# Narrow expert pieces: two groups of columns share a PSUM bank and one operation

## The chip, the cores and the metric

The kernel runs on one core of a Trainium2 chip. The metric is the device time of one execution in microseconds (us); the median of three runs before the change is 583.29 us (580.64 to 585.85). TensorE is called PE here, VectorE DVE, ScalarE ACT, GpSimd POOL; SP issues most of the DMAs.

## The reference

Three stages follow each other. First, attention inside chunks of 64 tokens, for 2 batches, 8 heads, 576 tokens and head size 64; its output is 1152 tokens of 512 numbers. Second, a mixture of 8 experts: each token goes to the one expert with the largest logit, at most 288 tokens to an expert, and gets `gate * (relu(x @ w1[e]) @ w2[e])` with w1 of 512x1024 and w2 of 1024x512. Third, a dense mixture of 4 domains: every token gets the sum over domains of `p[e] * (relu(x @ w1[e]) @ w2[e])`, with weights of the same sizes.

```
for i in range(N):
    e = expert_idx[i]
    if counts[e] < capacity:
        disp[e, counts[e]] = x[i]
...
h = np.maximum(np.einsum('ecd,edf->ecf', disp, w1), 0.0)
y = np.einsum('ecf,efd->ecd', h, w2)
```

With the inputs of these runs the 8 experts get 0, 210, 384, 0, 64, 174, 192 and 128 tokens.

## The kernel before, in words

All products are made from two parts of each number: a rounded high part and the remainder (low part). ACT writes the high part and DVE subtracts it from the number to get the remainder. For weights these are `part_hi` (L113, ACT, a cast of 128x1024) and `part_lo` (L117, DVE, a subtraction of 128x1024); a weight matrix half is one of four buffers `raws[j]`, `hls[j]`, each handled in two halves. Buffers 0 and 2 hold the two halves of w1, buffers 1 and 3 those of w2. So each expert costs eight casts on ACT and eight subtractions on DVE, and SP reloads a half of `raws` as soon as its subtraction is done.

The experts are worked one after another, as pieces, largest first, and each piece has a width in columns (tokens). Widths above 192 go through `wide`, with three matmuls for each product; widths 192 and 128 go through `joined`, where one matmul streams the high and low parts side by side (two halves of a bank) and a second adds the product of the weights' remainder. In these runs there are two wide pieces (k = 0 and 1), two pieces of width 192 (k = 2 and 3) and two of width 128 (k = 4 and 5). The last two are the narrow pieces. Then the dense stage begins with `first_dense` (L732 to L736) and takes most of the span.

A joined piece has a first layer of 8 groups of 4 matmul pairs (w1) and a second of 4 output groups with two halves each, 8 steps of 4 matmul pairs (w2). For each finished group `join` copies one half of the bank out on ACT (L626) and adds the other on DVE (L627), and `leave` clips the sum on ACT (L632) and takes the remainder on DVE (L633); in the second layer `leave` splits the result into `x2` (L546, L547). A result is left one group later than it is joined. Six banks rotate over the groups.

The order of the instructions on PE, ACT, DVE and SP is written out by hand. `chores` fills numbered slots, one after each of the 16 steps of a piece: `part_hi`, `part_lo` and `load` for the weights to come, `turn` (four PE transposes of the next expert's tokens into `tps`) and `split` (L546, L547 on them). Each engine executes its own list in order. Branches on the counted sizes choose the form of each next piece, so ACT and DVE jump to another piece of code when the form changes.

Of the kernel before, what the change touches and what calls it, by code (L numbers as in the profile page):

```python
# [20 lines left out]
P = 128  # L21
# [49 lines left out]
def kernel(ctx: ExitStack, tc: tile.TileContext, kqv_d, wg, w_all, dp, cst, out, cap):  # L71
# [461 lines left out]
    with ExitStack() as est:  # L533
# [8 lines left out]
        parts = [xtp.tile([P, CW], F32, name=f"part{j}") for j in range(3)]  # L542
        sums = [xtp.tile([P, CW], F32, name=f"sum{j}") for j in range(3)]
# [62 lines left out]
        def joined(k, W, slots):  # L606
# [5 lines left out]

            def bank(i):
                return banks[(first + i) % NB][:, 0:2 * W].rearrange("p (a n) -> p a n", a=2)
# [9 lines left out]
            def join(i):  # L624
                o, part, total = bank(i), parts[i % 3][:, 0:W], sums[i % 3][:, 0:W]
                nc.scalar.copy(part, o[:, 1])  # L626
                nc.vector.tensor_tensor(out=total, in0=o[:, 0], in1=part, op=ALU.add)  # L627

            def leave(i):
                total = sums[i % 3][:, 0:W]  # L630
                if i < NH * NF:
                    nc.scalar.activation(out=ht[:, i, 0], in_=total, func=ACTF.Relu)  # L632
                    nc.vector.scalar_tensor_tensor(out=ht[:, i, 1], in0=total, scalar=0.0, in1=ht[:, i, 0].bitcast(F32),  # L633
                                                   op0=ALU.max, op1=ALU.subtract)
                else:
                    d = i - NH * NF
                    hi_lo(x2[:, 0, d, cols], x2[:, 1, d, cols], total)

            def out(i):
                if i < last:  # L640
                    join(i)
                if i in range(1, last + 1) and i != NH * NF:
                    leave(i - 1)
# [7 lines left out]
            leave(NH * NF - 1)  # L651
            for h in range(NH):
                for d in range(KD):
                    for j in range(NF):
                        products(bank(NH * NF + d), lambda a: w2(h, a, j)[:, d * P:d * P + P], ht[:, NF * h + j],
                                 h == 0 and j == 0, h == NH - 1 and j == NF - 1)
                    if h == NH - 1:
                        out(NH * NF + d)
                    place(NH * NF + h * KD + d)
            leave(last - 1)  # L660

        def late(k):

            for h in range(2):
                part_hi(1, h)
# [351 lines left out]
```

## Time and profile before

| | |
|---|---|
| median of 3 runs | 583.29 us (580.64 to 585.85) |
| the profiled execution | 581.8 us, of which span 580.0 us |
| attention and routing | 0 to 64.6 us of the span |
| wide pieces, k = 0 and 1 | 64.6 to 117.8 us |
| pieces of 192 columns, k = 2 and 3 | 117.8 to 158.4 us |
| narrow pieces, k = 4 and 5 | 158.4 to 195.1 us |
| dense stage | 195.1 to 580 us |
| busy share of the span | PE 96%, DVE 53%, ACT 33% |

The boundaries are the starts of the first matmul of each piece in PE's order of time. PE is busy for nearly all of the span, so a change shows in the time where PE stands still, or where its clock is low.

### The profile page before, as it was taken

To read this page: it belongs to the slowest core of one execution; us is meant where nothing else is said; L and a number is where in the kernel's file an instruction comes from. 1 tells how busy PE (TensorE), PEld (TensorE's weight loads), DVE (VectorE), ACT (ScalarE), POOL (GpSimd) and SP (SyncE) were. 2 spreads that over 40 slices of the span, in tenths; PEclk is the share of its full clock that TensorE was granted. 3 is DMA by queue.
4 is the path that set the end of the run, shared out by engine and by line. 5 is a ranking of instruction groups with operands and counts; after the bars stand their busy time and mean duration, and the time that the engine had idled before them with its cause. 6 is when DMAs were issued, how large, how long until landed. Compare 5 with 4: busy or idle time off the path is not lost.

```text
span 580.0 us, 9331 instructions
## 1 busy us (share of the span) xinstructions
PE 557.7 (96%) x3627; PEld 510.3 (88%) x3627; DVE 305.2 (53%) x657; ACT 192.8 (33%) x429; POOL 64.3 (11%) x57
## 2 busy tenths in 40 slices
PE   7999799999989899999999999999999999999994
PEld 4786699999978788898898899899899889889984
DVE  5998576569868744334433524524533533453221
ACT  5785135568767541022122122122111212211110
POOL 3321805401103000000000000000000000000032
PEclk9999899999999899999999999999999999999999
DMA  8881394657748824011201202101210000000022
GB/s 333 316 289 62 87 366 149 201 177 250 239 147 273 257 66 160 1 37 41 69 3 70 73 0 73 56 18 38 73 36 2 1 0 1 0 1 1 1 92 76
DMA packets 17012, 59.99 MB, mean 103 GB/s; under 512 B 2768, under 2 KB 2912, under 8 KB 16288
## 3 DMA queue, kind: packets, MB, share of 16 engines
q1 hardware_dynamic: 14688, 52.91, 26.9%
q0 software_dynamic: 2240, 6.09, 3.2%
q8 instruction: 37, 0.61, 0.4%
q14 instruction: 47, 0.39, 0.2%
HBM read 54.25 MB, written 4.75 MB: 102 GB/s over the span
## 4 chain that ended last, share of the span: by engine, by line
PE 86%; DVE 6%; issue 3%; DMA 1%; ACT 1%; POOL 1%; SPq 0%; POOLq 0%; DVEq 0%; ACTq 0%
PE pg L863 31%; PE po L892 22%; PE po L911 9%; PE bank L579 9%; PE bank L617 5%; PE bank L618 2%; DVE hl L117 2%; PE bank L732 2%; PE w_ps L143 1%; PE s_ps L212 1%; DMA kqv<-in_kqv 1%; PE tp L552 1%; PE o_ps L234 1%; PE lr_ps L262 1%; DVE sum L627 1%
## 5 line engine op out<-in xcount | busy, mean ns | idle before, releaser
L863 PE MATMUL pg<-x,hl 128*128 128x384 f32 (+1 forms) x1104 | 181.1, 323 | 1.3 <-DVE htb L735 1.3
L863 PEld LDWEIGHTS pg<-x,hl 128*128 128x128 f32 x1104 | 178.0, 188 | 2.8 <-ACT htb L734 1.6
L117 DVE TENSOR_TENSOR hl<-raw,hl 128x1024 fp32r<-128x1024 f32 x80 | 96.8, 1220 | 8.7 <-ACT hl L113 8.7
L113 ACT CAST hl<-raw 128x1024 fp32r<-128x1024 f32 x80 | 82.0, 1049 | 4.1 <-issue 3.0
L892 PE MATMUL po<-hl,htb 128*128 128x512 f32 x288 | 68.4, 395 | 0.0
L892 PE MATMUL po<-hl,h_other 128*128 128x512 f32 (+1 forms) x300 | 68.4, 386 | 0.0
L892 PEld LDWEIGHTS po<-hl,h_other 128*128 128x128 f32 x300 | 54.6, 188 | 11.8
L892 PEld LDWEIGHTS po<-hl,htb 128*128 128x128 f32 x288 | 53.9, 188 | 12.1
L899 DVE SCALAR_TENSOR_TENSOR xr<-po,mcol,xr 128x512 f32<-128x512 f32 (+1 forms) x43 | 31.7, 738 | 58.2 <-PE po L892 57.5
L873 ACT ACTIVATE h_other<-pg 128x384 fp32r<-128x384 f32 x32 | 15.5, 490 | 90.1 <-PE pg L863 90.1
L873 ACT ACTIVATE htb<-pg 128x384 fp32r<-128x384 f32 x28 | 13.7, 491 | 87.0 <-PE pg L863 87.0
L874 DVE SCALAR_TENSOR_TENSOR h_other<-pg,h_other 128x384 fp32r<-128x384 f32 x32 | 17.6, 557 | 43.7 <-ACT h_other L873 43.7
L874 DVE SCALAR_TENSOR_TENSOR htb<-pg,htb 128x384 fp32r<-128x384 f32 x28 | 15.6, 558 | 43.7 <-ACT htb L873 43.7
L617 PE MATMUL bank<-htb,hl 128*128 128x384 f32 (+1 forms) x128 | 35.9, 355 | 0.1
L617 PE MATMUL bank<-xt,hl 128*128 128x384 f32 (+1 forms) x128 | 33.8, 348 | 1.9 <-DVE xt L547 1.0
L618 PE MATMUL bank<-htb,hl 128*128 128x192 f32 (+1 forms) x128 | 30.7, 240 | 1.2 <-DVE hl L117 1.2
L407 POOL DMA_INDIRECT xr<-x_d,gidx x18 | 21.5, 1195 | 85.5 <-PE tp L552 62.4
L920 POOL MEMSET raw<- 128x512 f32 x1 | 0.5, 525 | 272.8 <-DVE hl L117 272.8
L618 PE MATMUL bank<-xt,hl 128*128 128x192 f32 (+1 forms) x128 | 30.3, 237 | 0.0
L579 PE MATMUL bank<-xt,hl 128*128 128x232 f32 (+1 forms) x192 | 25.4, 296 | 2.9 <-issue 2.9
L579 PEld LDWEIGHTS bank<-xt,hl 128*128 128x128 f32 x192 | 25.1, 202 | 3.0 <-issue 3.0
L917 DVE TENSOR_TENSOR rest<-po,rest 128x288 f32<-128x288 f32 x28 | 12.8, 457 | 26.7 <-PE po L911 26.7
(174 smaller groups left out, 694.8 us busy)
## 6 DMA issues: line engine op xcount, KB each, us to landing
raw<-in_w_all SPq DMA_DIRECT2D x72, 512.0 KB, 4.7
kqv<-in_kqv SPq DMA_DIRECT2D x8, 768.0 KB, 7.6
raw<-in_w_all SPq DMA_DIRECT2D x4, 1024.0 KB, 5.5
x_d<-x SPq DMA_DIRECT2D x9, 256.0 KB, 2.8
xt<-meta_d SPq DMA_DIRECT2D x1, 1056.0 KB, 8.8
kqv<-in_kqv SPq DMA_DIRECT2D x3, 256.0 KB, 2.9
ca<-in_cst SPq DMA_DIRECT2D x1, 320.0 KB, 7.8
xr<-x_d,gidx POOLq DMA_INDIRECT x18, 5.5
```

What stands on the lines that cost most here:

```text
L113: nc.scalar.copy(hls[j][:, 0, a:b], raws[j][:, a:b])
L117: nc.vector.tensor_tensor(out=hls[j][:, 1, a:b], in0=raws[j][:, a:b], in1=hls[j][:, 0, a:b].bitcast(F32), op=ALU.subtract)
L407: nc.gpsimd.indirect_dma_start(out=xrs[k % 2][0:n, w, :], out_offset=None, in_=x_d[:, :], in_offset=bass.IndirectOffsetOnAxis(ap=ix, axis=0))
L579: nc.tensor.matmul(o, wt(a), t[:, b, 0:W], start=start and i == 0, stop=stop and i == len(PAIRS) - 1, skip_group_check=True)
L617: nc.tensor.matmul(o, wt(0), t[:, :, 0:W], start=start, stop=False, skip_group_check=True)
L618: nc.tensor.matmul(o[:, 0], wt(1), t[:, 0, 0:W], start=False, stop=stop, skip_group_check=True)
L863: nc.tensor.matmul(pg[:, 0:n], w1(u % 2, a, kd)[:, ff * P:ff * P + P], x2[:, b, kd, g * GW:g * GW + n], start=c == 0, stop=c == 3 * KD - 1)
L873: nc.scalar.activation(out=h[:, ff, 0], in_=pg[:, 0:GW], func=ACTF.Relu)
L874: nc.vector.scalar_tensor_tensor(out=h[:, ff, 1], in0=pg[:, 0:GW], scalar=0.0, in1=h[:, ff, 0].bitcast(F32), op0=ALU.max, op1=ALU.subtract)
L892: nc.tensor.matmul(po, h[:, ff, a, tt * P:tt * P + P], w2(u % 2, b, ff)[:, cols], start=c == 0, stop=c == 3 * NF - 1)
L899: nc.vector.scalar_tensor_tensor(out=acc[t][:, cols], in0=po, scalar=pe, in1=acc[t][:, cols], op0=ALU.mult, op1=ALU.add)
L911: nc.tensor.matmul(po[:, 0:W], w2(u % 2, b, ff)[:, d * P:d * P + P], h[:, ff, a, 0:W], start=c == 0, stop=c == 3 * NF - 1)
```

## The change

For pieces of 128 columns (`DW`), `joined` is called with m = 2: two groups of columns are put into one PSUM bank, and one copy, one sum, one clip and one remainder serve both, on 128x256 elements. So a narrow piece uses its six banks once each. The next expert's transposes are done two at a time into one bank, and their split is one operation for both (`turn2`, `split2`). Since two groups of the second layer lie in one bank, its eight steps get another order. For pieces of 192 columns (m = 1) `joined` computes as before. In every piece but the first, the casts and subtractions of the w2 halves are put into other slots: casts after steps 0, 1, 3 and 5 where they stood after 0, 2, 5 and 7, subtractions after 0, 2, 4 and 6 where they stood after 1, 3, 6 and 8.

```diff
-            def join(i):
-                o, part, total = bank(i), parts[i % 3][:, 0:W], sums[i % 3][:, 0:W]
-                nc.scalar.copy(part, o[:, 1])
-                nc.vector.tensor_tensor(out=total, in0=o[:, 0], in1=part, op=ALU.add)
+                nc.scalar.copy(kept(parts, i), half(i, 1))
+                nc.vector.tensor_tensor(out=kept(sums, i), in0=half(i, 0), in1=kept(parts, i), op=ALU.add)
...
             def out(i):
-                if i < last:
-                    join(i)
-                if i in range(1, last + 1) and i != NH * NF:
-                    leave(i - 1)
+                if (i + 1) % m:
+                    return
+                i += 1 - m
+                join(i)
+                if i and i != NH * NF:
+                    leave(i - m)
...
+            steps = [(h, d) for h in range(NH) for d in range(KD)]
+            if m > 1:
+                steps = [(0, 0), (0, 2), (1, 0), (0, 1), (1, 1), (1, 2), (0, 3), (1, 3)]
...
+            def turn2(kd):
+                for i in range(2):
+                    xturn(k + 1, kd + i, tps[kd // 2][:, i * W:], W)
+
+            def split2(kd):
+                t = tps[kd // 2][:, 0:2 * W].rearrange("p (b n) -> p b n", b=2)
+                hi_lo(*(xts[(k + 1) % 2][:, kd:kd + 2, a, 0:W] for a in range(2)), t)
+
+            if k + 1 < NE and W == DW:
+                for kd in (0, 2):
+                    at(7 + kd, turn2, kd)
+                    at(8 + kd, split2, kd)
...
-                    at((0, 2, 5, 7)[n], part_hi, j, h)
-                    i = (1, 3, 6, 8)[n]
+                    at((0, 1, 3, 5)[n], part_hi, j, h)
+                    i = (0, 2, 4, 6)[n]
```

How the instructions move on DVE, at the start of a narrow piece. `sum` rows are joins, `htb` rows are the remainders of the clipped result, `hl1` and `hl3` rows are the subtractions for the two halves of w2. Before:

```order
L627 TENSOR_TENSOR sum0_1054<-bank0_1042,part0_1051 128x128
L627 TENSOR_TENSOR sum1_1055<-bank1_1043,part1_1052 128x128
L633 SCALAR_TENSOR_TENSOR htb_1035<-sum0_1054,htb_1035 128x128
L117 TENSOR_TENSOR hl1_94<-raw1_90,hl1_94 128x1024
L627 TENSOR_TENSOR sum2_1056<-bank2_1044,part2_1053 128x128
L633 SCALAR_TENSOR_TENSOR htb_1035<-sum1_1055,htb_1035 128x128
L627 TENSOR_TENSOR sum0_1054<-bank3_1045,part0_1051 128x128
L633 SCALAR_TENSOR_TENSOR htb_1035<-sum2_1056,htb_1035 128x128
L117 TENSOR_TENSOR hl1_94<-raw1_90,hl1_94 128x1024
L627 TENSOR_TENSOR sum1_1055<-bank4_1046,part1_1052 128x128
```

And now:

```order
L117 TENSOR_TENSOR hl1_94<-raw1_90,hl1_94 128x1024
L635 TENSOR_TENSOR sum0_1054<-bank0_1042,part0_1051 128x256
L117 TENSOR_TENSOR hl1_94<-raw1_90,hl1_94 128x1024
L635 TENSOR_TENSOR sum1_1055<-bank1_1043,part1_1052 128x256
L642 SCALAR_TENSOR_TENSOR htb_1035<-sum0_1054,htb_1035 128x2x128
L117 TENSOR_TENSOR hl3_96<-raw3_92,hl3_96 128x1024
L635 TENSOR_TENSOR sum2_1056<-bank2_1044,part2_1053 128x256
L642 SCALAR_TENSOR_TENSOR htb_1035<-sum1_1055,htb_1035 128x2x128
L117 TENSOR_TENSOR hl3_96<-raw3_92,hl3_96 128x1024
L635 TENSOR_TENSOR sum0_1054<-bank3_1045,part0_1051 128x256
L642 SCALAR_TENSOR_TENSOR htb_1035<-sum2_1056,htb_1035 128x2x128
L642 SCALAR_TENSOR_TENSOR htb_1035<-sum0_1054,htb_1035 128x2x128
```

A weight subtraction now stands ahead of the first join, and all four of them stand among the first layer's four joins and four remainders.

On DVE at the end of a narrow piece, after the first layer's last remainder (`xt1` rows are the split of the next expert's tokens, `hl0` and `hl2` the next expert's w1, `x2` rows the piece's result). Now:

```order
L547 TENSOR_TENSOR xt1_1050<-tp0_1048,xt1_1050 128x2x128
L117 TENSOR_TENSOR hl0_93<-raw0_89,hl0_93 128x1024
L547 TENSOR_TENSOR xt1_1050<-tp1_1049,xt1_1050 128x2x128
L117 TENSOR_TENSOR hl0_93<-raw0_89,hl0_93 128x1024
L635 TENSOR_TENSOR sum1_1055<-bank4_1046,part1_1052 128x256
L117 TENSOR_TENSOR hl2_95<-raw2_91,hl2_95 128x1024 x2
L635 TENSOR_TENSOR sum2_1056<-bank5_1047,part2_1053 128x256
L547 ISA
L547 TENSOR_TENSOR x2_1032<-sum1_1055,x2_1032 128x2x128
L547 ISA
L547 TENSOR_TENSOR x2_1032<-sum2_1056,x2_1032 128x2x128
```

Before, this stretch held four splits of the tokens, four joins and four splits of the result, and the last split of the tokens stood behind the third split of the result. The next expert's tokens are now complete before the piece's first output group is joined.

## Rows read from the trace of the kernel before

**Rows 1.** Windows of the narrow pieces: engine busy times, PEclk (1.00 is full), DMA.

```profile
158.40:177.90 19.50, 16.81 (x134) 15.68 (x134) 14.26 (x33) 12.55 (x33) 1.29 (x1) 1.00 0.55 175
177.90:195.10 17.20, 15.75 (x134) 15.27 (x134) 15.26 (x37) 13.43 (x37) 4.57 (x3) 1.00 0.88 254
```

**Rows 2.** Timeline of PE, 158 to 212 us: its waits; start, length, instruction, idle.

```profile
165.16 0.38 PE L617 MATMUL bank<-xt,hl 128*128 128x256 f32 x1 [0.94 <-DVE sum L627]
...
169.11 0.33 PE L618 MATMUL bank<-htb,hl 128*128 128x128 f32 x1 [0.75 <-DVE hl L117]
...
173.50 0.33 PE L552 MATMUL tp<-cc,xr 128*128 128x128 f32 x1 [0.70 <-DVE xt L547]
...
179.78 0.36 PE L617 MATMUL bank<-xt,hl 128*128 128x256 f32 x1 [1.01 <-DVE xt L547]
...
196.23 1.31 PE L732 MATMUL bank<-x,hl 128*128 128x384 f32 x6 [0.71 <-DVE x L547]
...
198.42 9.01 PE L732 MATMUL bank<-x,hl 128*128 128x384 f32 x41 [0.88 <-DVE x L547]
```

**Rows 3.** Timeline of PE in the first narrow piece: two first matmuls, 21 pairs apart.

```profile
158.92 0.34 PE L617 MATMUL bank<-xt,hl 128*128 128x256 f32 x1
...
163.82 0.34 PE L617 MATMUL bank<-xt,hl 128*128 128x256 f32 x1
```

**Rows 4.** Timeline of ACT and DVE where the code changes form (k = 1 to 2, 3 to 4).

```profile
121.12 0.32 ACT L626 COPY part<-bank 128x192 f32<-128x192 f32 x1 [2.66 <-PE bank L618]
...
160.28 0.35 ACT L546 CAST x<-sum 128x192 f32 x1 [0.96 <-DVE sum L627]
...
160.66 0.36 DVE L547 TENSOR_TENSOR x<-sum,x 128x192 f32 x1 [0.16 <-ACT x L546]
...
164.01 0.27 ACT L626 COPY part<-bank 128x128 f32<-128x128 f32 x1 [3.38 <-PE bank L618]
...
164.82 0.29 DVE L627 TENSOR_TENSOR sum<-bank,part 128x128 f32<-128x128 f32 x1 [3.79 <-ACT part L626]
```

**Rows 5.** Groups by line and form: count, busy us, mean ns of one, idle before.

```profile
L117 DVE TENSOR_TENSOR hl<-raw,hl 128x1024 fp32r<-128x1024 f32 x80 | 96.8, 1220 | 8.7 <-ACT hl L113 8.7
L113 ACT CAST hl<-raw 128x1024 fp32r<-128x1024 f32 x80 | 82.0, 1049 | 4.1 <-issue 3.0 <-DMA raw<-in_w_all 1.1
...
L627 DVE TENSOR_TENSOR sum<-bank,part 128x128 f32<-128x128 f32 x24 | 6.9, 287 | 6.5 <-ACT part L626 6.5
...
L243 DVE TENSOR_TENSOR x<-o_ps,rs 128x256 f32<-128x256 f32 x18 | 6.8, 419 | 0.3
...
L256 ACT COPY xt<-et_ps 128x256 f32<-128x256 f32 x1 | 0.4, 378 | 0.0
```

**Rows 6.** Timeline of DVE: starts of operations that follow each other without idle time.

```profile
22.48 0.76 DVE L243 TENSOR_TENSOR x<-o_ps,rs 128x256 f32<-128x256 f32 x2
...
172.95 0.29 DVE L633 SCALAR_TENSOR_TENSOR htb<-sum,htb 128x128 fp32r<-128x128 f32 x1 [0.18 <-ACT htb L632]
...
177.16 0.28 DVE L547 TENSOR_TENSOR xt<-tp,xt 128x128 fp32r<-128x128 f32 x1
177.36 1.22 DVE L117 TENSOR_TENSOR hl<-raw,hl 128x1024 fp32r<-128x1024 f32 x1
178.49 0.29 DVE L627 TENSOR_TENSOR sum<-bank,part 128x128 f32<-128x128 f32 x1
```

**Rows 7.** Windows around PE's idle stretches; columns as in Rows 1.

```profile
61.60:64.60 3.00, 0.13 (x3) 0.02 (x2) 1.55 (x4) 1.31 (x4) 2.96 (x2) 1.00 0.42 126
64.60:69.00 4.40, 4.37 (x24) 4.40 (x25) 1.67 (x3) 0.36 (x1) 4.29 (x1) 0.61 0.04 9
...
200.00:202.00 2.00, 2.00 (x8) 2.00 (x7) 0.56 (x1) 0.49 (x1) 0.00 (x0) 0.53 0.95 371
```

**Rows 8.** Timeline of ACT: the last two groups of the first dense layer.

```profile
205.36 0.49 ACT L734 ACTIVATE htb<-bank 128x384 fp32r<-128x384 f32 x1 [1.62 <-PE bank L732]
...
207.46 0.49 ACT L734 ACTIVATE htb<-bank 128x384 fp32r<-128x384 f32 x1 [1.61 <-PE bank L732]
```

More of the change, by code (lines that the diff above doesn't have):

```diff
@@ L541 @@
                for x in (xt0, xtp.tile([P, 2 * KD * XW], F32R, name="xt1"))]
-        parts = [xtp.tile([P, CW], F32, name=f"part{j}") for j in range(3)]
-        sums = [xtp.tile([P, CW], F32, name=f"sum{j}") for j in range(3)]
+        parts = [xtp.tile([P, 2 * DW], F32, name=f"part{j}") for j in range(3)]
+        sums = [xtp.tile([P, 2 * DW], F32, name=f"sum{j}") for j in range(3)]
         def hi_lo(hi, lo, src):
@@ L604, in wide, with joined @@
                     place(NH * NF + h * KD + d)
-        def joined(k, W, slots):
+        def joined(k, W, slots, m):
             xk, ht = xts[k % 2], held(W)
@@ L611, in joined, with group, half, kept @@
             last = NH * NF + KD
+            def group(i):
+                return banks[(first + i) // m % NB][:, 0:2 * m * W].rearrange("p (b a n) -> p b a n", b=m, a=2)
             def bank(i):
-                return banks[(first + i) % NB][:, 0:2 * W].rearrange("p (a n) -> p a n", a=2)
+                return group(i)[:, i % m]
+            def half(i, a):
+                return group(i)[:, :, a]
+            def kept(x, i):
+                return x[i // m % 3][:, 0:m * W].rearrange("p (b n) -> p b n", b=m)
             def products(o, wt, t, start, stop):
@@ L650, in joined @@
                 place(ff)
[L651 to L660, printed above, removed]
-        def late(k):
-            for h in range(2):
-                part_hi(1, h)
-                part_lo(1, h)
-                load(k + 1, 1, h)
-            for h in range(2):
-                part_hi(3, h)
-                part_lo(3, h)
-                load(k + 1, 3, h)
+            leave(NH * NF - m)
+            steps = [(h, d) for h in range(NH) for d in range(KD)]
+            if m > 1:
+                steps = [(0, 0), (0, 2), (1, 0), (0, 1), (1, 1), (1, 2), (0, 3), (1, 3)]
+            for n, (h, d) in enumerate(steps):
+                for j in range(NF):
+                    products(bank(NH * NF + d), lambda a: w2(h, a, j)[:, d * P:d * P + P], ht[:, NF * h + j],
+                             h == 0 and j == 0, h == NH - 1 and j == NF - 1)
+                if h == NH - 1:
+                    out(NH * NF + d)
+                place(NH * NF + n)
+            leave(last - m)
+        def late(k):
+            for j in (1, 3):
+                for h in range(2):
+                    part_hi(j, h)
+                    part_lo(j, h)
+                    load(k + 1, j, h)
         def hint(label, off):
@@ L690, in known @@
                 regs[:] = numbers(pli[0:1, :], engines=(ENG.SP,), max_val=NE + NDOM - 1)
-            if k + 1 < NE:
+            def turn2(kd):
[8 more added lines that the diff above has]
+                    at(8 + kd, split2, kd)
+            elif k + 1 < NE:
                 for kd in range(KD):
@@ L752, in small_from @@
                 ahead(k + 1, CW)
-                joined(k, CW, chores(k, True, known, CW))
+                joined(k, CW, chores(k, True, known, CW), 1)
                 small_from(k + 1, tag)
@@ L768, in least_from @@
                 ahead(k + 1, DW)
-                joined(k, DW, chores(k, True, known, DW))
+                joined(k, DW, chores(k, True, known, DW), 2)
                 least_from(k + 1, tag)
```

10 lines of the change are left out of this document (5 added, 5 removed).

## The prediction

> **What bounds the kernel now.** I read the share of busy time first, then the windows of the pieces, then PE's own order of time, and last DVE's and ACT's order around PE's waits. PE is busy for 96% of the span, so a change of DVE's and ACT's work can only win what PE loses in the narrow pieces: they take 19.5 and 17.2 us [rows 1]. A matmul pair there starts every 0.233 us (21 pairs from 158.92 to 163.82) [rows 3]; 64 pairs are 14.9 us, and with the four transposes of the next expert a piece that never waits takes about 15.3 us. So the two pieces lose 4.2 and 1.9 us. The waits are seen in PE's order of time [rows 2]: at 165.16 for the sum that frees a bank, at 169.11 for a weight remainder, at 173.50 and 179.78 for a split of the tokens. The first dense layer then starts at 195.1, but stands until 196.23 and again until 198.42, for the last piece's results.
>
> [...] Where the form changes from 192 to 128 columns, ACT does nothing for 3.38 us and DVE for 3.79 us, though their inputs are long there: ACT's first copy starts at 164.01, DVE's first sum at 164.82 [rows 4]. I read this as the time to get the code of the new form. From then on DVE runs nearly without a gap to the end of the pieces. [...]
>
> **What the operations cost.** What counts on DVE is not the length of an operation but how far apart two starts are. A 128-column operation is 0.287 us long [rows 5], and the next starts 0.20 us later; the 1024-column subtraction is 1.22 us long with 1.13 us to the next; two 256-column operations in a row take 0.76 us, the second 0.42 long [rows 5, 6], so 0.34 apart. A narrow piece has 28 short operations and 8 subtractions now: 28 x 0.20 + 8 x 1.13 = 14.6 us. After the change it has 14 of twice the width: 14 x 0.34 + 9.0 = 13.8 us. So the joining saves only 0.8 us of DVE in a piece. The joined operand lies in two runs of 128 columns. I take 0.34, because the row it comes from (L243) reads four runs of 64 columns out of PSUM, and bound it by 0.57, two full lengths of 0.287 with no overlap, and by 0.27, twice the 0.132 us that 128 more columns add.
>
> [...]
>
> **First narrow piece, step by step.** PE starts at 158.4 as before, since the pieces of 192 columns are not held by DVE and their slots only move forward. With two groups to a bank the first layer fits into four banks, so the wait at 165.16 goes: 32 pairs and two transposes end at 166.1. DVE begins later than before, though: its first operation is now a subtraction that needs ACT's cast of 1.05 us [rows 5], from 164.0 to 165.1. From there four subtractions, four sums and four remainders are 4 x 1.13 + 8 x 0.34 = 7.2 us, and the last remainder waits about 0.25 more for its clip. It is ready at 172.7, where before it was ready at 173.24 [rows 6]. The new order of the second layer asks for it earlier: two steps (1.9 us) after the first layer instead of four (3.7 us). So PE idles about 3.7 of the 4.2 us from 166.1 to 170.4, once for the first remainders and once for the second, and half a step and five steps remain after 172.7: 0.5 + 5 x 0.93 = 5.1 us, end 177.8, against 177.9. The piece wins nothing: the wait for a bank becomes a wait for the clipped result.
>
> Such an idle stretch has lowered the clock before: PE did 0.13 us of work in the 3.0 us before 64.6, and the clock was 0.61 in the 4.4 us behind it [rows 7]. I expect that here too, at up to 1.8 us, of which some 0.7 falls into the waits that are there anyway. The piece then ends near 178.9.
>
> **Second narrow piece.** ACT and DVE change no code here, and the tokens are split by 175, so the wait of 1.01 us at 179.78 goes. DVE is done with the first piece at 180.0 to 180.6. Its 13.8 us, with 0.9 us of waits for casts and clips, end at 195.3 to 195.9. PE runs 64 pairs, transposes and about 0.2 us of waits: 178.9 + 15.4 = 194.3. This stage goes from bound by DVE to nearly even.
>
> **Start of the dense stage.** Both output pairs are left only after the last step: copy 0.38 [rows 5], sum, split. The first pair is ready at 195.4, the second 0.5 us later, and the first six matmuls (1.05 us at 0.175) cover that. So PE idles 1.1 us once, instead of 1.8 us in two parts within 3.3 us, and I expect the clock to stay. Four groups at 2.10 us end at 195.4 + 8.4 = 203.8. Before, the last clip starts at 207.46 [rows 8], so PE is done at 207.4. **The sum** is 3.6 us, about half of it clock. I take everything behind to move by that, since PE then runs on for the rest of the span. Weight loads leave SP when a subtraction ends, in order; four a piece leave earlier, and 4.2 MB in 15.4 us is 272 GB/s, where the second piece moved 254 [rows 1].
>
> The moved slots in the wide and 192-column pieces I cost at nothing: PE's work covers them; if the cover went, one subtraction of 1.22 us would stand on the path.
>
> Against the profiled execution (581.8 us, span 580.0) this is 578.2; the median of the runs shown is 1.5 above it, so I say 579.7.
>
> **The rivals.**
> 1. The clock falls at the start of the dense stage as it does now. For: the total idle is not much smaller. Against: it is one stretch of 1.1 us, and the clock stayed through 0.94 and 0.75 us waits [rows 1, 2]. It takes 1.8 us back: 581.5. Chance 0.18.
> 2. Joined operations save their full lengths: 14 x (2 x 0.287 - 0.419) = 2.2 us a piece instead of 0.8 [rows 5], as where each waits for another engine and none overlaps. Then DVE frees 1.4 us more in each piece; the first ends earlier, but the second meets PE's own 15.3 us, so some 1.7 us more: 578.0. Chance 0.10. [...]
> 3. The code arrives sooner. ACT's other change of form cost 2.66 us instead of 3.38 [rows 4]; by 0.7 to 1.3 us the whole chain moves: 578.7. [...] Chance 0.11.
> 4. **Slower:** the two-run operand costs like two operations, in the sums and splits of the narrow pieces. At 0.57 instead of 0.34, 28 operations add 6.4 us to DVE's chain, which sets the end: 2.8 slower, 586.1. It decides from 0.47 us on. For: the sums of before read one run of columns. Against: L243 reads four runs in 0.42 us [rows 5]. Chance 0.06.
> 5. The change does not shorten anything, since weights arrive too late for the quicker second piece, or waits for clips add up: 583.3. For: DMA share 0.88 in that piece [rows 1]. Against: ACT's casts wait for DMA 1.1 us in all [rows 5]. Chance 0.08.
>
> **Numbers.** The forecast has 0.47, with the rivals 1.00. The range 576.5 to 584.5 takes in cases 1, 2, 3 and 5 and about 1.5 us of spread of a median, and leaves out most of case 4. About 1% (5.8 us) is what a measurement here can tell from no change. Faster by that needs cases 2 and 3 together, or a lucky run: 0.13. Slower by it needs case 4 and more: 0.06. Within: 0.81.
>
> **What would show it.** In the changed profile: 256-column sums 0.42 us long and 0.34 apart; no wait of PE for a sum in the first layer; a wait of over 2 us before the first step of the second layer in the first narrow piece, and a granted clock under 1 behind it; no wait at the start of the second; the first dense matmuls after 195 us at full clock; pieces of 19.5 to 20.5 and about 15.4 us. It is wrong if the first piece shrinks by over 1 us, if the sums take 0.47 or more, or if pieces of 192 columns change by over 0.5 us.

## The result, and the profile after

The changed kernel takes 587.76 us (median of 4 runs, 587.09 to 590.80) where the kernel before takes 582.03 in the same set: ratio 1.0115, 95% interval 1.0083 to 1.0148. It is slower by about 1%. The forecast was 579.7, range 576.5 to 584.5. The profiled execution took 587.41 us, span 585.6.

First the windows of the stages, from one piece's first matmul to the next one's, with the columns of [rows 1]; ahead of them two windows of the kernel before that were not shown yet, the second wide piece and the dense start.

```profile
90.12:117.80 27.68, 27.68 (x206) 26.85 (x205) 16.29 (x28) 13.68 (x24) 14.71 (x12) 1.00 0.56 184
...
195.12:207.40 12.28, 10.69 (x50) 9.82 (x49) 5.21 (x13) 3.37 (x10) 0.00 (x0) 0.86 0.55 193
```

The changed kernel: both wide pieces, one of 192 columns, both narrow ones, dense start, and two shorter stretches.

```profile
64.93:90.37 25.44, 25.44 (x205) 24.57 (x205) 19.11 (x48) 9.21 (x20) 7.51 (x4) 0.94 0.68 243
90.37:124.56 34.19, 31.62 (x206) 29.60 (x205) 16.10 (x28) 13.46 (x24) 11.98 (x12) 0.90 0.51 148
124.56:144.90 20.34, 20.34 (x139) 19.48 (x137) 16.23 (x34) 14.72 (x34) 1.95 (x2) 1.00 0.64 204
...
165.25:187.56 22.31, 18.73 (x134) 18.35 (x133) 14.96 (x25) 12.13 (x22) 3.56 (x3) 0.85 0.63 208
187.56:203.12 15.56, 15.56 (x133) 15.21 (x133) 13.82 (x23) 12.12 (x22) 1.38 (x2) 1.00 0.83 241
203.12:213.40 10.28, 9.14 (x50) 8.46 (x49) 3.81 (x7) 2.56 (x6) 0.00 (x0) 1.00 0.49 161
...
106.00:112.00 6.00, 5.67 (x24) 5.14 (x24) 5.00 (x8) 4.13 (x7) 0.00 (x0) 0.50 0.45 124
...
177.00:184.00 7.00, 6.67 (x31) 6.67 (x32) 5.62 (x9) 4.19 (x7) 1.61 (x1) 0.52 0.77 240
```

The loss stands where nothing was forecast: the second wide piece takes 34.2 us instead of 27.7 (+6.5). The first narrow piece takes 22.3 instead of the 19.4 of before (+2.9), the second and the dense start 25.8 instead of 29.5 (-3.7). Behind it both kernels take the same time: from the last matmul of the first dense layer to the end of the span it is 372.9 us before and 372.6 after.

**The second wide piece.** PE's order of time in the changed kernel; its 96 first-layer matmuls stand in one row of 12.86 us in the kernel before.

```profile
90.37 11.41 PE L579 MATMUL bank<-xt,hl 128*128 128x288 f32 x85
102.20 0.53 PE L579 MATMUL bank<-xt,hl 128*128 128x288 f32 x2 [0.42 <-issue]
102.92 0.29 PE L579 MATMUL bank<-xt,hl 128*128 128x288 f32 x1 [0.19 <-issue]
103.63 0.40 PE L579 MATMUL bank<-xt,hl 128*128 128x288 f32 x1 [0.42 <-issue]
104.37 0.52 PE L579 MATMUL bank<-xt,hl 128*128 128x288 f32 x2 [0.34 <-issue]
105.75 0.40 PE L579 MATMUL bank<-xt,hl 128*128 128x288 f32 x1 [0.87 <-issue]
106.48 1.12 PE L579 MATMUL bank<-xt,hl 128*128 128x288 f32 x4 [0.33 <-issue]
107.40 0.87 PE L552 MATMUL tp<-cc,xr 128*128 128x128 f32 x3
```

And ACT's order of time there; behind it one row of the view of its line L591 (the clip of the first layer), on the waits of its queue: count, least, median and longest in ns.

```profile
95.39 0.41 ACT L591 ACTIVATE htb<-bank 128x288 fp32r<-128x288 f32 x1 [0.22 <-issue]
97.96 0.41 ACT L591 ACTIVATE htb<-bank 128x288 fp32r<-128x288 f32 x1 [2.16 <-PE bank L579]
98.27 1.04 ACT L113 CAST hl<-raw 128x1024 fp32r<-128x1024 f32 x1
105.11 0.41 ACT L591 ACTIVATE htb<-bank 128x288 fp32r<-128x288 f32 x1 [5.81 <-issue]
```

```profile
L591 ACTq EVENT_SEMAPHORE  x7: 17/1468/7060, 92.2 to 106.7; - x7
```

Groups of 12 matmuls are clipped every 1.58 us until 95.39. The fourth is clipped at 97.96 instead of 96.97, the fifth at 105.11 instead of 98.5, though by PE's own row 60 matmuls at 0.132 us were under way by 98.3. ACT spent 7.06 us of this in one semaphore wait, so the profile's "issue" is wrong here: the signal of the fifth group came 6.6 us late. From 102 us on PE itself slows down: seven matmuls take 4.28 us (102.20 to 106.48), 0.6 us each. So PE's transposes behind the first layer start 17.0 us after the piece's start instead of 12.7: 4.3 us. The clock then falls to 0.50 (window 106.00:112.00), and the second layer takes 17.2 us instead of 15.0: 2.2 us. Together that is the 6.5.

**The narrow pieces.** DVE's order of time (its first operation, a joined sum, a clip remainder, the last remainder of the first layer), which answers [rows 4 to 6].

```profile
172.12 1.23 DVE L117 TENSOR_TENSOR hl<-raw,hl 128x1024 fp32r<-128x1024 f32 x1 [4.34 <-ACT hl L113]
...
174.73 0.41 DVE L635 TENSOR_TENSOR sum<-bank,part 128x256 f32<-128x256 f32 x1
175.07 0.41 DVE L642 SCALAR_TENSOR_TENSOR htb<-sum,htb 128x256 fp32r<-128x256 f32 x1
175.40 1.21 DVE L117 TENSOR_TENSOR hl<-raw,hl 128x1024 fp32r<-128x1024 f32 x1
...
179.23 0.42 DVE L642 SCALAR_TENSOR_TENSOR htb<-sum,htb 128x256 fp32r<-128x256 f32 x1 [0.15 <-ACT htb L641]
```

PE's waits from 165 to 212 us, in place of the six of [rows 2].

```profile
175.53 0.38 PE L626 MATMUL bank<-htb,hl 128*128 128x256 f32 x1 [2.45 <-DVE htb L642]
...
177.34 0.58 PE L626 MATMUL bank<-htb,hl 128*128 128x256 f32 x1 [1.13 <-DVE htb L642]
...
204.26 0.41 PE L753 MATMUL bank<-x,hl 128*128 128x384 f32 x1 [0.91 <-ACT x L546]
204.89 8.52 PE L753 MATMUL bank<-x,hl 128*128 128x384 f32 x47 [0.22 <-DVE x L547]
```

Two waits of 2.45 and 1.13 us stand at the start of the second layer, with 0.7 us of work between them, and then 6.8 us at half clock. The second narrow piece has no wait, and the dense start two, of 0.91 and 0.22 us, at full clock.

### The profile page after: what moved, and what is told of

It reads as the page before. It is cut to its first block, busy times and chain, and to the rows that moved or that the text cites. A ratio compares the mean times of both kernels' runs of the same rounds, so it can differ in the third digit from the quotient of the medians.

```text
span 585.6 us, 9258 instructions
## 1 busy us (share of the span) xinstructions
PE 563.1 (96%) x3627; PEld 515.0 (88%) x3627; DVE 303.1 (52%) x629; ACT 190.0 (32%) x401; POOL 59.7 (10%) x57
## 4 chain that ended last, share of the span: by engine, by line
PE 87%; DVE 4%; issue 3%; ACT 2%; DMA 1%; POOL 0%; SPq 0%; POOLq 0%; DVEq 0%; ACTq 0%
PE pg L884 30%; PE po L913 21%; PE bank L579 9%; PE po L932 9%; PE bank L626 6%; PE bank L627 2%; PE bank L753 1%; PE tp L552 1%; PE w_ps L143 1%; PE s_ps L212 1%; DMA kqv<-in_kqv 1%; DVE hl L117 1%; PE o_ps L234 1%; PE lr_ps L262 1%; ACT hl L113 1%
## 5 line engine op out<-in xcount | busy, mean ns | idle before, releaser
L894 ACT ACTIVATE htb<-pg 128x384 fp32r<-128x384 f32 x28 | 13.8, 492 | 87.0 <-PE pg L884 87.0
L626 PE MATMUL bank<-htb,hl 128*128 128x384 f32 (+1 forms) x128 | 38.3, 377 | 3.6 <-DVE htb L642 3.6
L579 PE MATMUL bank<-xt,hl 128*128 128x232 f32 (+1 forms) x192 | 27.2, 301 | 5.6 <-ACT xt L546 3.0
L579 PEld LDWEIGHTS bank<-xt,hl 128*128 128x128 f32 x192 | 25.8, 203 | 6.7 <-issue 3.6
L626 PEld LDWEIGHTS bank<-htb,hl 128*128 128x128 f32 x128 | 26.2, 204 | 4.9 <-DVE htb L642 4.2
L407 POOL DMA_INDIRECT xr<-x_d,gidx x18 | 19.8, 1099 | 92.7 <-PE tp L552 69.6
```

The source lines that it names most:

```text
L407: nc.gpsimd.indirect_dma_start(out=xrs[k % 2][0:n, w, :], out_offset=None, in_=x_d[:, :], in_offset=bass.IndirectOffsetOnAxis(ap=ix, axis=0))
L579: nc.tensor.matmul(o, wt(a), t[:, b, 0:W], start=start and i == 0, stop=stop and i == len(PAIRS) - 1, skip_group_check=True)
L626: nc.tensor.matmul(o, wt(0), t[:, :, 0:W], start=start, stop=False, skip_group_check=True)
L894: nc.scalar.activation(out=h[:, ff, 0], in_=pg[:, 0:GW], func=ACTF.Relu)
```

## The experiments

The table gives all runs beside the kernel before of the same set. The three columns on the right are from the profiled execution: second wide piece, first narrow piece, second narrow piece with the first dense layer, in us (each from first matmul to first matmul, the last one to the start of the last dense matmul).

| kernel | median us (runs) | ratio, 95% interval | wide | 1st narrow | 2nd + dense |
|---|---|---|---|---|---|
| before | 582.03 (4) | | 27.68 | 19.43 | 29.17 |
| changed | 587.76 (4) | 1.0115 (1.0083-1.0148) | 34.20 | 22.31 | 25.51 |
| e1 slots only | 580.08 (10) | 0.9972 (0.9947-0.9998) | 27.68 | 19.13 | 27.30 |
| e2 old slots | 581.52 (10) | 0.9985 (0.9952-1.0017) | 27.68 | 21.81 | 26.11 |
| e3 old slots wide | 580.55 (10) | 0.9989 (0.9965-1.0014) | 27.68 | 21.38 | 25.11 |
| e4 tiles only | 583.03 (10) | 1.0002 (0.9961-1.0044) | 27.68 | 19.45 | 29.17 |
| e5 changed | 587.84 (7) | 1.0098 (1.0066-1.0130) | 33.13 | 22.12 | 25.10 |
| e6 join later | 585.92 (10) | 1.0062 (1.0034-1.0090) | 32.98 | 20.32 | 26.59 |
| e7 filled | 586.21 (10) | 1.0051 (1.0025-1.0076) | 33.03 | 19.95 | 25.34 |
| e8 slots, tiles | 582.80 (10) | 0.9997 (0.9962-1.0031) | 27.68 | 19.11 | 27.30 |
| e9 no scatter | 579.95 (10) | 0.9967 (0.9930-1.0004) | 27.68 | 22.13 | 25.11 |
| e10 later, old wide | 580.09 (10) | 0.9966 (0.9927-1.0006) | 27.68 | 19.22 | 26.95 |
| e11 filled, old wide | 579.08 (10) | 0.9959 (0.9921-0.9996) | 27.69 | 19.67 | 25.34 |
| e12 changed | 589.00 (5) | 1.0073 (1.0049-1.0098) | 32.77 | 22.05 | 25.11 |
| e13 slots only | 586.98 (10) | 1.0042 (1.0022-1.0061) | 32.57 | 19.07 | 28.84 |
| e14 one later | 579.42 (4) | 0.9910 (0.9881-0.9939) | 27.68 | 21.67 | 25.10 |
| e15 no scatter | 580.43 (5) | 0.9931 (0.9904-0.9959) | 27.69 | 21.27 | 25.11 |
| e16 load later | 586.52 (10) | 1.0074 (1.0050-1.0098) | 33.89 | 21.95 | 25.11 |
| e17 one later, filled | 580.30 (10) | 0.9959 (0.9928-0.9990) | 27.68 | 19.40 | 25.36 |
| e18 changed | 587.50 (9) | 1.0084 (1.0058-1.0111) | 33.97 | 22.45 | 25.11 |

Sets on one chip each: e1 to e4, e5 to e7, e8 to e11, e12 to e15, e16 to e18. The kernel before has medians of 581.96, 582.14, 581.86, 584.33 and 582.59 us in them. The first, third and fifth set ran on a chip listed under the same number.

Totals are a rougher measure than stages here. In the twenty profiles the second wide piece starts between 89.6 and 95.1 us, behind code that no edit touches, while the time from the last dense matmul to the end is always 372.0 to 373.2 us. The argument therefore goes by the stages.

### The parts alone: e1 to e4

e1 makes one edit in the kernel before:

```diff
-                    at((0, 2, 5, 7)[n], part_hi, j, h)
-                    i = (1, 3, 6, 8)[n]
+                    at((0, 1, 3, 5)[n], part_hi, j, h)
+                    i = (0, 2, 4, 6)[n]
```

> The kernel before with one part of the change alone: the casts, subtractions and loads of the second layer's weight halves at the even distances (0,1,3,5 and 0,2,4,6), in the wide and 192-column pieces and in the narrow ones. Nothing is joined in the narrow pieces. Theory A (the moved slots make TensorE lose 6.7 us in the second wide piece): the piece takes about 34 us instead of 27.7, clock 0.5 behind the loss, total about 588 us (585 to 590). Theory B (the wider tiles of the partial sums, which move what lies behind them in SBUF): piece 27.7 us, total 580 to 584. Theory C (neither alone; the two together, or the place of code): also 580 to 584, and the run with the tiles alone is unchanged too.

e2 takes this edit back in the changed kernel, in every piece.

> The changed kernel with the old distances of the weight halves (0,2,5,7 and 1,3,6,8) in every piece; the joined groups of two columns stay, and so do the wider tiles. Theory A: the second wide piece is back at 27.7 us and the total is about 581 us (579 to 583), the joining alone being worth 0 to 2 us. Theory B: 586 to 589 us, the piece at 34 us as in the changed kernel. Theory C leaves both open.

e3 takes it back where `W > CW`, that is in the wide piece alone.

> The changed kernel with the old distances in the wide piece alone (288 columns); the pieces of 192 and 128 columns keep the new ones. Theory A: 581 us (579 to 583), the second wide piece at 27.7 us, the narrow ones as in the changed kernel (about 21 and 18 us). Theory B: 586 to 589 us.

e4 makes the tiles wider in the kernel before:

```diff
-        parts = [xtp.tile([P, CW], F32, name=f"part{j}") for j in range(3)]
-        sums = [xtp.tile([P, CW], F32, name=f"sum{j}") for j in range(3)]
+        parts = [xtp.tile([P, 2 * DW], F32, name=f"part{j}") for j in range(3)]
+        sums = [xtp.tile([P, 2 * DW], F32, name=f"sum{j}") for j in range(3)]
```

> The kernel before with nothing but the six tiles of the partial sums widened from 192 to 256 columns, as in the changed kernel; no instruction differs but for addresses. Theory A: no change, 580 to 584 us. Theory B: the second wide piece takes 34 us and the total is 586 to 589 us. Theory C: no change.

None of the four has the loss, and no kernel that has it ran beside them. e1 says that on this chip the slots aren't enough for it. e2, e3 and e4 fit a need for the slots of the wide piece, but on a chip where e1 has no loss they can't show it. e3 against e1 also shows what joining does by itself: the second narrow piece with the dense start gains 2.19 us (27.30 to 25.11), and the first narrow piece gives 2.25 back (19.13 to 21.38). So e3, which is the change without its loss in the wide piece, isn't clearly faster than the kernel before (0.9965 to 1.0014).

### The changed kernel again, and its first narrow piece: e5 to e7

e5 is the changed kernel, unaltered.

> The changed kernel itself, unaltered, timed again beside the kernel before. The kernel with the new distances alone and the one with the old distances in the wide piece alone both had the second wide piece at 27.7 us and came to 580 to 581 us. Theory D (the loss in that piece belongs to the changed kernel as a whole): again 34 us for the piece, 586 to 590 us. Theory E (it belongs to the occasion of that one measurement, not to the program): 27.7 us for the piece, clock there 1.00, total 580 to 582 us.

The loss is there again (33.13 us), so theory E falls.

e6 leaves the first narrow piece in the old form:

```diff
-        def chores(k, small, ahead, W=XW):
+        def chores(k, small, ahead, W=XW, m=1):
...
-            if k + 1 < NE and W == DW:
+            if k + 1 < NE and m > 1:
...
-                least_from(k, f"{tag}_{k}")
+                least_from(k, f"{tag}_{k}", 1)
-        def least_from(k, tag):
+        def least_from(k, tag, m=2):
...
-                joined(k, DW, chores(k, True, known, DW), 2)
+                joined(k, DW, chores(k, True, known, DW, m), m)
```

> The changed kernel with the first narrow piece in the old form (one group of columns at a time, four separate splits, the second layer in the old order), at the new distances; only the second narrow piece joins two groups. If joining costs time in the first narrow piece because TensorE then waits 4 us in one place and its clock falls, the first narrow piece takes 19 to 19.5 us without a half-clock stretch, the second with the dense groups 25 to 26 us, and the total is 577.5 to 579.5 us, below both kernels, if the second wide piece is undisturbed (584 if it isn't). If joining helps as much in the first narrow piece as in the second, it is slower than the changed kernel.

A miss for my first case: the piece takes 20.3 us and still has half a clock (mean 0.83) behind a wait of 2.03 us for a sum. Joining is not the only way to such a wait. In e10 (below) the same code of this piece has waits of 1.01, 0.47, 0.53 and 0.92 us instead, and keeps its clock (1.00). DVE's first sum shows the difference: behind ACT's copy it comes 1.0 us later in e6 than in e10, and the profile shows nothing else that it waits for. First e6, then e10:

```profile
170.04 0.27 ACT L634 COPY part<-bank 128x128 f32<-128x128 f32 x1 [3.51 <-PE bank L627]
...
171.81 0.29 DVE L635 TENSOR_TENSOR sum<-bank,part 128x128 f32<-128x128 f32 x1 [4.88 <-ACT part L634]
```

```profile
164.83 0.27 ACT L634 COPY part<-bank 128x128 f32<-128x128 f32 x1 [3.48 <-PE bank L627]
...
165.59 0.29 DVE L635 TENSOR_TENSOR sum<-bank,part 128x128 f32<-128x128 f32 x1 [3.86 <-ACT part L634]
```

This is DVE's idle time where the code changes form, which thus differs by 1 us between two executions.

e7 fills the wait with work, in the first narrow piece only (`fill` is 10 there and 0 elsewhere):

```diff
+            for i in range(fill):
+                nc.tensor.matmul(tps[1], wz[:, 0:P], wz, start=True, stop=True)
             if m > 1:
                 steps = [(0, 0), (0, 2), (1, 0), (0, 1), (1, 1), (1, 2), (0, 3), (1, 3)]
```

> The changed kernel with ten matmuls of zeros (512 columns each, some 2.2 us) into a bank that nobody reads, ahead of the second layer of the first narrow piece, where TensorE waits 2.7 us for the first clipped sum. If the half-clock stretch that follows (6.8 us long in the changed kernel) comes from that idle time, the clock stays at 1.0 and the piece falls from 21.4 or 22.3 us to about 18.5 to 19.5; total 2 to 3 us below the changed kernel timed beside it. If the clock falls for another reason, the piece stays at 21 to 22.5 us and the total is unchanged.

The clock stays at 1.00 and the piece takes 19.95 us. So the half clock there is the price of the idle time in front of it, and it is 2.2 us (22.12 - 19.95); e18 against e17, below, gives 3.05 (22.45 - 19.40).

### What the loss needs: e8 to e11

e8 is e1 and e4 together.

> The kernel before with the new distances and the wider tiles of partial sums, nothing joined: its instructions up to the end of the second wide piece are those of the changed kernel, and so are its tile addresses; what differs is the code of the later pieces, and with it where code lies. Alone, neither part disturbed the second wide piece (27.7 us each). If the addresses of the tiles together with the new distances make TensorE stall there, the piece takes 33 us and the total is 585 to 588 us. If it is the place of the code or something else that the joined pieces bring, the piece stays at 27.7 us and the total at 580 us.

27.68 us: on this chip the tiles add nothing to the slots.

e9 replaces GpSimd's seven indirect writes:

```diff
-            scatter(meta_d, [(posi[:, i:i + 1], meta[:, i]) for i in range(NT)], [])
+            nc.gpsimd.dma_start(out=meta_d.rearrange("(i p) c -> p i c", p=P), in_=meta)
```

> The changed kernel with GpSimd's seven indirect writes of the tokens' data replaced by one plain transfer of the same bytes, so that these rows land in the order of the tokens and not of the experts (this part of the computation is left out). In the changed kernel these seven writes run without a gap from 92.1 to 100.8 us, and TensorE's signals to the other engines come late from 97 us on; in the kernels without the stall two of them, and one of the gathers behind, are stretched to 1.6 to 2.0 us by VectorE's subtractions. If the writes have a part in the stall, the second wide piece falls from 33 or 34 to 27.7 us and the total to 579 to 582 us. If they only stand beside it (code, tiles, the weight loads alone), it stays at 33 us and the total at 585 to 588 us.

27.68 us, but beside e8, which has no loss either; e15 repeats it beside the changed kernel.

e10 is e6 with the edit of e3, e11 is e7 with the edit of e3.

> The changed kernel with the old distances in the wide piece and the first narrow piece not joined. No stall in the second wide piece (27.7 us), first narrow piece 19 to 20.5 us, the second narrow with the dense groups 25 to 26.6 us: 577 to 580 us, 2 to 4 us below the kernel before. If what the first narrow piece loses does not hang on joining, 580 to 582 us.

> The changed kernel with the old distances in the wide piece and the ten matmuls of zeros ahead of the second layer of the first narrow piece. With them the first narrow piece took 19.95 us at the full clock, against 22.1 us with 6.8 us at half clock. No stall in the second wide piece (27.7 us), first narrow piece 18.5 to 20 us without a half-clock stretch, the rest as in the changed kernel (25 us): 577.5 to 579.5 us, some 2 us below the same kernel without the zeros (580.6 us, timed on another chip). If the clock falls all the same, 580 to 581 us.

e10 came to 580.1, just above what I expected of it, with 26.95 us in the last column instead of 25 to 26.6. e11 came as expected: 579.1, no half clock in the pieces, and below the kernel before.

### Distances, writes and the chip: e12 to e15

e12 is the changed kernel, e13 is e1, e15 is e9, all beside each other.

> The changed kernel itself, beside the kernel with the new distances alone, on one chip. Theory F (the stall of the second wide piece needs the new distances there and GpSimd's seven writes, and it needs the joined kernel's code as well): 33 to 34 us for the piece, 586 to 589 us. Theory G (it needs the distances and the writes, and decides by the chip it runs on, since the kernels with and without the stall were timed on different chips): the changed kernel and the kernel with the distances alone agree with each other, both at 33 us (586 to 589 us) or both at 27.7 us (580 to 582 us).

> The kernel before with the new distances alone, beside the changed kernel on one chip. Theory F: 27.7 us for the second wide piece, about 580 us. Theory G: the same length of this piece as the changed kernel has on this chip; 586 to 588 us where it stalls.

> The changed kernel with one plain transfer in place of the seven indirect writes (their rows land in another order; that part of the computation is left out), on the chip on which the changed kernel runs beside it. If the writes have a part in the stall, 27.7 us for the second wide piece and 579 to 582 us where the changed kernel has 33 us and 586 to 589; if the chip alone decided before, both have the same length.

e14 moves one subtraction of the wide piece, and the load behind it, back by one group:

```diff
-                    i = (0, 2, 4, 6)[n]
+                    i = (int(W > CW), 2, 4, 6)[n]
```

> The changed kernel with one subtraction of the wide piece moved back by one group: the first weight half of the second layer is subtracted and its successor loaded at distance 1 (as before) instead of 0; the other three stay at 2, 4 and 6. In the kernel before, this subtraction holds up GpSimd's third write (1.98 us instead of 0.98) and the load comes behind it; in the changed kernel it lies ahead of that write, which is not held up, and the load's packets, from 5.5 us after the start of the piece on, take 1.1 us each instead of 0.2. If this meeting is what starts the stall, it goes: piece 27.7 us, total 580 to 582 us. If any other of the moved halves does it, 33 us and 585 to 589 us. On a chip where the changed kernel doesn't stall it tells nothing: 27.7 us.

The windows of the second wide piece, one line each of e1, e13, e14 and e15:

```profile
90.98:118.67 27.69, 27.69 (x207) 26.86 (x205) 16.34 (x28) 13.77 (x24) 13.21 (x12) 1.00 0.65 185
```

```profile
94.56:127.13 32.57, 30.22 (x207) 28.64 (x205) 16.17 (x28) 13.47 (x24) 11.96 (x12) 0.95 0.53 156
```

```profile
91.88:119.53 27.65, 27.65 (x206) 26.82 (x205) 16.27 (x27) 13.77 (x24) 14.51 (x12) 1.00 0.65 185
```

```profile
95.10:122.80 27.70, 27.70 (x206) 26.87 (x206) 16.37 (x28) 13.67 (x24) 7.23 (x7) 1.00 0.59 183
```

One program, with the distances alone, has the loss on one chip (e13) and not on another (e1): theory F falls, joining isn't needed, nor are the wider tiles. Theory G holds as far as this. Without the indirect writes, or with one subtraction and its load moved back, the loss is gone on the chip where the changed kernel has it. The kernel before, which differs from e13 by the distances alone, is faster there (e13: 1.0022 to 1.0061), so the distances are needed.

GpSimd's and DVE's order of time show what that subtraction does. The kernel before:

```profile
93.16 0.98 POOL L512 DMA_INDIRECT meta_d<-meta,posi  x1 [0.30 <-issue]
...
94.38 1.21 DVE L117 TENSOR_TENSOR hl<-raw,hl 128x1024 fp32r<-128x1024 f32 x1
...
94.45 1.98 POOL L512 DMA_INDIRECT meta_d<-meta,posi  x1 [0.30 <-issue]
```

The changed kernel:

```profile
93.41 0.98 POOL L512 DMA_INDIRECT meta_d<-meta,posi  x1 [0.30 <-issue]
...
93.62 1.23 DVE L117 TENSOR_TENSOR hl<-raw,hl 128x1024 fp32r<-128x1024 f32 x1 [0.41 <-ACT hl L113]
...
94.69 0.99 POOL L512 DMA_INDIRECT meta_d<-meta,posi  x1 [0.30 <-issue]
```

And e14:

```profile
96.12 1.22 DVE L117 TENSOR_TENSOR hl<-raw,hl 128x1024 fp32r<-128x1024 f32 x1
...
96.20 1.98 POOL L512 DMA_INDIRECT meta_d<-meta,posi  x1 [0.30 <-issue]
98.48 1.27 POOL L512 DMA_INDIRECT meta_d<-meta,posi  x1 [0.30 <-issue]
```

A write that starts 0.07 or 0.08 us behind a subtraction's start takes 1.98 us instead of 0.98, and ends 0.84 us behind the subtraction's end, as if it stood while the subtraction runs. In the changed kernel the second write starts 0.21 us ahead of the subtraction, and the third near its end; neither is held up, and all seven run at 0.97 to 1.01 us with 0.30 between them. In the kernel before and in e14 two or three of the seven take 1.3 to 2.0.

Where the write is first, the subtraction is hardly longer: 1.23 us against 1.21. In eight profiles PE loses 4.9 to 6.5 us in this piece. In the timelines of three of them, the changed kernel, e13 and e16, all seven writes run at 0.96 to 1.01 us. In these three and four more (e5, e7, e12, e18) GpSimd is busy for 11.95 to 11.98 us in the piece, against 13.21 to 14.71 in the kernel before, e1, e3, e8 and e14, which lose nothing. How the writes could reach PE is shown by no run here.

### Which side of the meeting: e16 to e18

e16 holds the first load back, not the subtraction:

```diff
                     at(i, part_lo, j, h)
-                    at(i, load, k + 1, j, h)
+                    if n or W <= CW:
+                        at(i, load, k + 1, j, h)
+                    if n == 1 and W > CW:
+                        at(i, load, k + 1, 1, 0)
```

> The changed kernel with the first load of the second layer's weights in the wide piece held back, so that it is issued right behind the second one (2.6 us later); the subtraction ahead of it stays at distance 0. GpSimd's third write is then not held up by that subtraction, as in the changed kernel, but no weight transfer starts beside it. If the stall comes from the writes running without a break, TensorE stalls here too: 32 to 34 us for the second wide piece, 586 to 589 us, as the changed kernel beside it. If it comes from the meeting of that transfer with the writes, 27.7 us and 580 to 582 us. Where the changed kernel beside it doesn't stall on this chip, it tells nothing.

e18 is its control, the changed kernel.

> The changed kernel, on the chip of the two others. Where it stalls, 32 to 34 us for the second wide piece and 586 to 589 us; where it doesn't, 27.7 us and 580 to 582 us.

Both have the loss (33.89 and 33.97 us). The load's meeting with the writes is not the cause. What is left is the place of the subtraction; that it acts through the unbroken run of writes is the likeliest reading, but no run spaced the writes in another way. And e18 has the loss on a chip listed under the number of e1 and e8, which have none: theory G, the chip alone, holds only if these are different chips.

e17 is e14 and e7 together. Beside e18 it repeats e14: its second wide piece takes 27.68 us.

> The changed kernel with both repairs: the first subtraction of the wide piece back at distance 1, and ten matmuls of zeros ahead of the second layer of the first narrow piece. Second wide piece 27.7 us on any chip, first narrow piece 19.5 to 20 us at full clock instead of 21.7, the second narrow with the dense groups 25.1 to 25.4 us: 1.5 to 2 us below the kernel with the first repair alone, 576.5 to 579 us where the kernel before takes 582 to 584 us, ratio 0.988 to 0.993. If the zeros cost what they fill, as the kernel with the first repair alone: ratio 0.991 to 0.996.

Its narrow pieces, both at full clock:

```profile
159.96:179.36 19.40, 18.15 (x144) 16.31 (x143) 14.49 (x25) 12.04 (x22) 1.72 (x2) 1.00 0.64 207
179.36:194.77 15.41, 15.41 (x134) 15.16 (x133) 14.14 (x23) 12.31 (x22) 2.79 (x3) 1.00 0.90 287
```

The stages are as expected: 19.40 and 25.36 us, 3.8 us less than in the profile of the kernel before. The total is not: ratio 0.9959 instead of 0.988 to 0.993. Its ten runs lie between 579.1 and 584.0 us with granted clocks from 0.995 to 0.983; only the one of 579.1 (0.995) left a profile, so where the others lose the rest is open; the start of the second wide piece, which varies by 5.5 us among the profiles, is the likely place.

**The best versions.** e14 is below the kernel before by 0.9% (interval 0.6 to 1.2) and the changed kernel beside it above by 0.7%. e17 and e11 are below by 0.4%. The 0.9% are 4.9 us, of which e14's stages explain 1.8; it has four runs, beside the highest median of the kernel before (584.33). Whether e14 or e17 is better isn't known; they ran on different chips.

## Why the prediction was wrong, step by step

- **The moved slots in the wide pieces, costed at nothing: this step failed.** I named PE's work as their cover, and one subtraction of 1.22 us as the price if it went. The cover held: PE never waited for the moved subtractions, and the pieces of 192 columns stayed at 20.3 us. But PE lost 6.5 us in the second wide piece, and with the first of these subtractions back in its old slot the loss is gone (e14, e17). What that subtraction does there is to hold up GpSimd's third write (1.98 us); moved, it doesn't (0.99 us), and the writes run through. I had followed who waits for a moved operation, and not whom it stops by running. None of the rivals had this; the slower one (the two-run operand) had another place and mechanism.
- **Costs of the joined operations: right.** The sums are 0.41 us long, and 0.34 us apart (174.73 to 175.07, and 175.40). Rivals 2 and 4 are out.
- **First narrow piece: right but for one size.** There is no wait for a sum in the first layer, and the two waits ahead of the second are 3.58 us against my 3.7. The last remainder starts 13.98 us after the piece's start; I had it ready at 14.3, and 13.98 + 0.42 is 14.4. I gave the clock 1.1 us there; it cost 2.2 (e7 against e5) to 3.05 (e17 against e18), as half clock lasted 6.8 us, so the piece took 22.31 us and not 20.5 (158.4 to 178.9). At full clock e17 has 19.40 us, which is my 158.4 to 177.8. The 1.8 us that I set for a lowered clock, there and in rival 1, was an estimate: 41 dense matmuls take 9.01 us in [rows 2], and 7.2 at the pitch of [rows 8]. The dense start takes 12.28 us in the kernel before (mean clock 0.86) and 10.62 in e1 (1.00).
- **Code of the new form: as assumed.** ACT's idle time at the change of form is 3.60 us, against 3.38 [rows 4]; rival 3 didn't happen. That it is the time to get the code stays my reading; beside it, the queue named "instruction" (q14) moves three packets within ACT's idle time in either kernel, from 162 to 163 us before and from 169 to 170 us now.
- **Second narrow piece: right.** 15.56 us without a wait, forecast 15.4.
- **Dense start: right but for 0.8 us.** Two waits of 1.1 us together, and the clock stays at 1.00. The matmuls end 10.3 us after the last narrow pair (203.12 to 213.4), forecast 9.5. Rival 1 is out: the mean clock there is 1.00, against 0.86 before. With a joined second narrow piece, the last column is 25.10 to 26.95 us in all fifteen profiles; without it, 28.84 to 29.17 in three (before, e4, e13) and 27.30 in two (e1, e8).
- **The sum.** I had 3.6 us for the narrow pieces and the dense start. The profile of the changed kernel has 0.8 (48.60 to 47.82, first narrow piece to last dense matmul), e14 has 1.8, and e17 3.8. So the gain was there, and half a clock in the first narrow piece kept most of it; the wide piece then took more than all. Part of the 48.60 may be luck: the clock falls at the dense start in the profile of the kernel before (0.86) but not in that of e1 (1.00), and e13, the same code as e1, has 28.84 us in the last column where e1 has 27.30.
- **Slips in the working.** DVE's end of the second piece comes to 194.7 to 195.3 by its terms (180.0 to 180.6, 13.8 and 0.9), not 195.3 to 195.9; nothing rests on it. The first piece's 3.7 us of waits and 15.3 of work end at 177.4, not 177.8. PE's two idle times at the old dense start are 0.71 and 0.88 us [rows 2], 1.6 together where I had 1.8.

**What is shown and what isn't.** Shown, each beside a kernel that has the loss on the same chip: the loss needs the new distances (e13 against the kernel before), of them the first subtraction and its load at distance 0 (e14, e17), and the indirect writes (e15). The place of the load alone doesn't matter (e16); joining and the wider tiles aren't needed (e13). e2, e3, e8 and e9 fit this, but had no kernel with the loss beside them. Not shown: that the subtraction acts through the writes that run unbroken; why the distances alone (e1, e8) escape on a chip listed under the number of the one where the changed kernel doesn't (e18), though their instructions up to there are the same and in the same order, and the first six writes run as unbroken in e1, at 0.97 to 1.01 us (its seventh takes 1.59); and by what way the writes reach PE. The seven writes' least, median and longest time in ns, in the changed kernel and then in e1:

```profile
L512 POOL DMA_INDIRECT meta_d<-meta,posi x7: 969/979/1008, 92.1 to 99.8; - x7
```

```profile
L512 POOL DMA_INDIRECT meta_d<-meta,posi x7: 969/985/1595, 92.7 to 100.5; - x7
```

The changed kernel's view of the transfers, 90 to 112 us, shows no time to landing for these writes. The last column, the median of it, is empty; before, it is 3.6 us.

```profile
meta_d<-meta,posi POOLq DMA_INDIRECT x7, 3.6
```

```profile
meta_d<-meta,posi POOLq DMA_INDIRECT x7
```

This doesn't tell the two cases apart: the column is empty in e13 and e16, which have the loss, and in e14 and e17, which don't; in e1, which doesn't, it is 4.9 us. Every time told here is of an execution that was recorded, so whether the loss exists without the recording isn't known either.

## What to carry to other kernels

When an operation moves, ask not only who waits for it but whom it holds up while it runs: a VectorE subtraction of 1.22 us held up one of GpSimd's writes (1.98 us instead of 0.99), and moving it away went with a loss of 6.5 us, five times its length. A kernel that does well only by such an accident of order is fragile; the same program had the loss on one chip (e13, 32.57 us) and not on another (e1, 27.68). And when waits are gathered together, price the clock with them: two waits of 2.45 and 1.13 us cost 2.2 to 3 us more in half clock, where four of at most 0.94 us left it at 1.00 (e1), and work of no use in place of the first won that back (e7: 19.95 us instead of 22.12).

## What the runs showed of the hardware

- An indirect write of GpSimd takes 0.98 us where no subtraction runs beside it (the second of the kernel before), and 1.98 us when it starts 0.07 or 0.08 us behind the start of a 128x1024 subtraction of 1.21 or 1.22 us (the third there and in e14).
- In the changed kernel seven such writes with 0.30 us between them go with signals of PE that come late by 1 us, then by over 6, and with PE at 0.6 us a matmul. Its four profiles, not all on one chip, lose 5.1 to 6.5 us in that piece, with GpSimd busy there for 11.95 to 11.98 us. Such writes don't always go with a loss: in e1 six run so (0.97 to 1.01 us) and the piece takes 27.68 us.
- The joined first narrow piece without the zeros takes 21.3 to 22.5 us in ten profiles. In the changed kernel, e3 and e14 it has a wait of 2.37 to 2.49 us, two pairs of matmuls, a wait of 0.69 to 1.13 us, and a mean clock of 0.84 or 0.85; the half clock lasts 6.8 us in the changed kernel. In the three with the zeros (e7, e11, e17) the first wait is at most 0.67 us, and the mean clock is 1.00.
- The length of a wait doesn't settle it alone: behind 0.71 and 0.88 us at the dense start the kernel before has a clock of 0.53 [rows 2, 7], and e17 keeps 1.00 in its first narrow piece with a wait of 1.13 us.
- In the changed kernel a semaphore wait of 7.06 us on ACT's queue stands in the profile as "issue" (5.81 us): the releaser of such an idle time has to be looked up in the view of its line.
